# A fused forgetting-attention and FFN kernel: FFN groups of 384 tokens with one bank for layer 1 and three for layer 2, and q and k in two halves of one tile

## The chip, the cores and the metric

The kernel runs on one core of a Trainium2 chip, as one launch. The metric is the device time of that launch in microseconds. The core's engines run side by side, each with its own queue in order: TensorE (PE; its weight loads are listed apart as PEld), VectorE (DVE), ScalarE (ACT), GpSimd (POOL) and SyncE (SP), which issues all DMAs here. TensorE writes its results into eight banks of PSUM, from which DVE and ACT read them.

## The reference, cut to what matters

```python
# q, k, v: (8, 8, 576, 64), f: (8, 8, 576); w_in: (512, 2048), w_out: (2048, 512), all float32
scores = (q @ k.T) / sqrt(64)
cum = cumsum(log(clip(f, 1e-4, 1)))
scores = where(causal, -1e9, scores + cum[:, None] - cum[None, :])
attn = exp(scores - max(scores)); attn = attn / (sum(attn) + 1e-9)
x = (attn @ v) as 4608 tokens of 512            # 8 heads side by side
h = x @ w_in
out = maximum(0.01 * h, h) @ w_out
```

Products are computed to more than one float32r pass: an operand is split into a high part (`..h`, rounded to float32r) and a low part (`..l`, the rest), and high·high, low·high and high·low are summed.

## The kernel before

**Attention.** The first 256 query rows of three batches are done in an early part, two heads at a time (`early_load`, `early_scores`, `early_values`), while the weights are loaded and split. Then 64 tasks follow, one for each head: for the three early batches the rest of the rows, for the five others all 576. The loop over `t` at line 704 does in one turn the scores of task `t` (line 375: matmuls into `sc`, a maximum on DVE, an exponential on ACT into a fixed tile `z0` to `z4`), and for task `t - 1` the transposes (line 417: PE into `tr`, ACT casts into `ph`, DVE subtracts into `pl`) and the values (line 482: matmuls into `av`, ACT copies one half of the partitions into `y`, DVE adds the other half to it into `x`). After every second task `inverse` (line 510) turns the sums of both heads into factors, sends them through DRAM (`rows_d`) and broadcasts them into `main` and `rest`, and `normalise` (line 534) multiplies `x` by both and stores it to `xd` in DRAM. `load(t + 1)` (line 240) fetches q, k and, for each pair of heads, v; q and k are loaded twice each, into both halves of the partitions of `qraw` and `kraw`. `split(t + 1)` (line 352) makes float32r tiles of them: `s1` and `m1` are cast on ACT, `s2` gets its upper half by a DMA out of `s1`, POOL subtracts (`minus`) for the low parts, and `vs` is made of `vm` in the same way. `qraw`, `kraw` and `vm` have one buffer each, `s1` and `m1` two.

**FFN.** The 4608 tokens are taken in 18 groups of 256 (`ffn`, line 574). A group is read back from `xd` (`fetch_group`), split (`split_group`), and then done in 8 steps `p`. A step is 2 x 12 layer-1 matmuls of 256 columns into one tile `h`, which takes a bank (2 buffers); ACT's Prelu makes `g` of it, DVE casts `gh`, POOL (DVE after the last task) subtracts `gl`; and `second` (line 625) does the 2 x 6 layer-2 matmuls of 512 columns of the step before into two accumulators `o0` and `o1`, a bank each.

**What sets the order.** The FFN is a generator that yields after each quantum: 12 layer-1 matmuls, or 6 of layer 2. `fill` (line 657) is called some 8 times in each turn of the task loop and draws quanta by a credit. How many a turn gets is set at lines 710 to 712: the quanta of the groups whose tokens are ready, less those used, over the turns to the next end of a batch plus 3, at most 9. A scheduler then orders each engine's instructions, and puts the waits in.

Of the kernel before, what the change touches and what calls it, by code (L numbers as in the profile page):

```python
# [19 lines left out]
PARTS = (("part0", 1), ("part1", 1), ("ost", 2), ("ost", 2))  # L20
# [17 lines left out]
def forgetting_attention_ffn(ctx, tc, qT, kT, v4, vr, f, w_in, w_out, out):  # L38
# [18 lines left out]
    NG = NTOK // T  # L57
# [66 lines left out]
    eye = one.tile([P, P], F32, tag="y", name="eye")  # L124
# [4 lines left out]
    both = one.tile([P, P + T + NHEAD], F32R, tag="kraw", name="both")  # L129
# [110 lines left out]
    def load(t):  # L240

        s, c0, c1 = tasks[t]
        h = state[t] = {}
        a, n = c0 * P, S
        for name, src, lo in (("q", qT, a), ("k", kT, 0)):
            x = h[name] = one.tile([P, S], F32, tag=f"{name}raw", name=f"{name}raw_{t}")
            for o in range(2):
                nc.sync.dma_start(x[o * D:(o + 1) * D, lo:n], src[s][:, lo:n])
# [87 lines left out]
    def fix():  # L336

        for x in "ab":
            for w, n in (("s2", 2), ("m2", 4)):
# [4 lines left out]
            nc.gpsimd.memset(y, 1.0)
        for i in range(NCH):
            z = fixed[f"z{i}"] = one.tile([P, (i + 1) * P], F32, tag=f"z{i}", name=f"fixed_z{i}")
            nc.gpsimd.memset(z if i == 0 else z[:, i * P + REST:], 0.0)
        vs = fixed["vs"] = one.tile([P, 2, NCH, 2 * D], F32R, tag="vs", name="fixed_vs")
        vm = fixed["vm"] = one.tile([P, 2, NCH, D], F32, tag="vm", name="fixed_vm")
        nc.gpsimd.memset(vm[:, :, NFULL], 0.0)  # L350

    def split(t):


        s, c0, c1 = tasks[t]
        h = state[t]
        a, n = c0 * P, S
        x = "ab"[t % 2]
        s1 = h["s1"] = one.tile([P, S], F32R, tag="s1", name=f"s1_{t}", bufs=2)
        m1 = h["m1"] = one.tile([P, S], F32R, tag="m1", name=f"m1_{t}", bufs=2)  # L360
        s2, m2 = h["s2"], h["m2"] = fixed["s2" + x], fixed["m2" + x]
        nc.scalar.copy(s1[:, a:n], h["q"][:, a:n])  # L362
        nc.scalar.copy(m1[:, :n], h["k"][:, :n])
# [9 lines left out]
        nc.gpsimd.tensor_copy(vs[REST:, NFULL], vs[:REST, NFULL].bitcast(F32))

    def scores(t, i):
# [9 lines left out]
        for x, (a, b) in enumerate(parts):  # L385
# [96 lines left out]
    def values(t, part):  # L482
# [12 lines left out]
        for n, (w, j) in enumerate(steps):  # L495
# [8 lines left out]
        y = one.tile([P, 512], F32, tag="y", name=f"y_{t}_{part}")  # L504
        nc.scalar.copy(y[mine, :hi - lo], ps[other, :hi - lo])
        nc.vector.tensor_tensor(
            x[mine, lo:hi], ps[mine, :hi - lo], y[mine, :hi - lo], op=ALU.add
        )

    def inverse(t):  # L510
# [10 lines left out]
        rest = one.tile([P, 2 * P], F32, tag="part1", name=f"rbr_{t}")  # L521
        flat = rest[:2 * NCH, P:]
# [51 lines left out]
    def ffn():  # L574
# [4 lines left out]
        for at, (n, p0, p1) in enumerate(order):  # L579
            while (n + 1) * T > ready[0]:  # L580
                yield False
            if n not in groups:
# [3 lines left out]
                while n not in groups:  # L586
                    yield False
            acc = [None, None]
            for p in range(p0, p1):
                while len(loaded) < 2 * (p + 1):  # L590
                    yield False
# [3 lines left out]
                    (x, c, w, xx) for c in range(NCC)  # L595
                    for x, (w, xx) in enumerate(((win_h[p], xh), (win_l[p], xh), (win_h[p], xl)))
# [13 lines left out]
                g = one.tile([P, 2, T], F32, tag="b2", name=f"g_{n}_{p}", bufs=B2)  # L610
                nc.scalar.activation(g, ph, AF.Prelu, alpha=0.01)  # L611
                gh = one.tile([P, 2, T], F32R, tag="b2", name=f"gh_{n}_{p}", bufs=B2)
                gl = one.tile([P, 2, T], F32R, tag="b2", name=f"gl_{n}_{p}", bufs=B2)
# [11 lines left out]
    def second(n, p, p0, p1, gh, gl, acc):
        for k in range(T // P):
            if p == p0:
                acc[k] = psum.tile([P, DM], F32, tag=f"o{k}", name=f"o_{n}_{k}_{p}", bufs=1)
            ts = slice(k * P, (k + 1) * P)
            for e in range(2):  # L630
                fc_ = 2 * p + e
                for x, (gg, w) in enumerate(((gh, wout_h[p]), (gh, wout_l[p]), (gl, wout_h[p]))):
                    matmul(
                        acc[k], gg[:, e, ts], w[:, e, :],
                        start=(fc_ == 2 * p0 and x == 0), stop=(fc_ == 2 * p1 - 1 and x == 2),
                    )
            if p == p1 - 1 < NFC // 2 - 1:
# [3 lines left out]
            elif p == p1 - 1:  # L641
# [15 lines left out]
    def fill(n):  # L657
# [17 lines left out]
    TRI = S  # L675
# [28 lines left out]
    for t in range(nt + 1):  # L704
# [5 lines left out]
        have = ready[0] // T * NQ - used[0]  # L710
# [60 lines left out]
```

## Time and profile before

| | |
|---|---|
| median of 3 runs | 1210.32 us (1210.28 to 1213.06) |
| the profiled execution | 1209.1 us |
| its span | 1207.3 us |
| TensorE busy | 1187.3 us, 98% of the span |
| DVE, ACT, POOL busy | 626.7, 631.6, 462.7 us |
| TensorE clock granted | full throughout |
| DMA engines | 92 GB/s in the mean |

Span and busy times are from the profiler on the chip. Matmuls are pipelined, and the ends shown for them overlap the starts of the next; the time that one takes from TensorE is read from start to start. A wait is put down to what came last.

### The profile page before, as it was taken

What the parts mean: (1) busy time and instruction counts of PE and PEld (TensorE: products, weight loads), DVE (VectorE), ACT (ScalarE), POOL (GpSimd) and SP (SyncE); (2) the same over time, 40 slices, a digit from 0 to 9 for tenths busy, and PEclk for the clock granted to TensorE, in tenths of its full rate; (3) what the DMA queues carried; (4) which work ended last, traced back from release to release, by engine and by line L of the source; (5) the groups of instructions that cost most, each with busy time, mean ns of one, the idle gap of its engine ahead of it and who ended that gap; (6) DMA issues with size and microseconds to landing.
All of it is one profiled execution on the core that took longest, in us unless ns stands there. A gap on an engine that the chain in (4) does not pass through costs nothing.

```text
span 1207.3 us, 22237 instructions
## 1 busy us (share of the span) xinstructions
PE 1187.3 (98%) x7812; PEld 1065.9 (88%) x7812; DVE 626.7 (52%) x1687; ACT 631.6 (52%) x1633; POOL 462.7 (38%) x471
## 2 busy tenths in 40 slices
PE   9899989999999999999999999999999999999998
PEld 6678878988899999999999999999999999899997
DVE  5988646666665554454544444445443434553221
ACT  6886446757765565555544545455444445551111
POOL 0000245664455444454445354444454543631000
PEclk9999999999999999999999999999999999999999
DMA  5555323334342233323322323231223222211000
GB/s 171 197 188 171 101 84 111 98 108 135 106 134 81 79 98 97 107 79 97 98 90 61 90 71 96 74 96 52 73 85 93 58 75 76 73 57 47 18 18 18
DMA packets 81104, 110.53 MB, mean 92 GB/s; under 512 B 19617, under 2 KB 50705, under 8 KB 80993
## 3 DMA queue, kind: packets, MB, share of 16 engines
q1 hardware_dynamic: 80992, 109.11, 29.6%
q8 instruction: 62, 1.02, 0.3%
q14 instruction: 50, 0.40, 0.1%
HBM read 82.62 MB, written 18.58 MB: 84 GB/s over the span
## 4 chain that ended last, share of the span: by engine, by line
PE 88%; DVE 4%; DMA 3%; ACT 2%; issue 1%; SPq 1%; POOL 1%; ACTq 0%; POOLq 0%; DVEq 0%
PE h L108 32%; PE o L108 30%; PE tr L112 8%; PE av L108 7%; PE sc L108 7%; PE sce L108 2%; PE warm L108 1%; PE ave L108 1%; DMA wraw<-in_w_in 1%; DMA qraw<-in_qT 1%; DMA kraw<-in_kT 1%; ACT fixed_z L399 1%; DVE fixed_z L393 1%; DVE pl L445 0%; ACT ph L443 0%
## 5 line engine op out<-in xcount | busy, mean ns | idle before, releaser
L616 POOL TENSOR_TENSOR gl<-g,gh 128x512 fp32r<-128x512 f32 x111 | 145.5, 1311 | 286.8 <-DVE gh L614 266.7
L108 PE MATMUL o<-wout_h,gh 128*128 128x512 f32 x576 | 230.3, 400 | 0.0
L108 PE MATMUL o<-wout_l,gh 128*128 128x512 f32 x576 | 226.3, 393 | 0.0
L108 PE MATMUL o<-wout_h,gl 128*128 128x512 f32 x576 | 225.6, 392 | 0.0
L399 ACT ACTIVATE fixed_z<-fixed_z,max 128x192 f32<-128x192 f32 (+3 forms) x272 | 161.0, 592 | 106.7 <-DVE max L393 103.3
L108 PE MATMUL h<-xh,win_h 128*128 128x256 f32 x1152 | 207.8, 286 | 0.4 <-ACT xh L331 0.4
L393 DVE CUSTOM_DVE_ANT_0 fixed_z<-sc,tri 128x192 f32<-128x192 f32 (+3 forms) x272 | 122.6, 452 | 151.0 <-PE sc L108 148.1
L108 PE MATMUL h<-xh,win_l 128*128 128x256 f32 x1152 | 200.4, 283 | 0.4 <-DVE win_l L190 0.4
L611 ACT ACTIVATE g<-h 128x512 f32<-128x512 f32 x144 | 85.8, 596 | 217.4 <-PE h L108 206.8
L443 ACT CAST ph<-tr 128x192 fp32r<-128x192 f32 (+3 forms) x360 | 126.3, 373 | 132.9 <-PE tr L112 97.3
L614 DVE CAST gh<-g 128x512 fp32r<-128x512 f32 x144 | 75.2, 522 | 204.2 <-ACT g L611 202.6
L445 DVE TENSOR_TENSOR pl<-tr,ph 128x384 fp32r<-128x384 f32 (+3 forms) x296 | 137.9, 468 | 78.1 <-ACT ph L443 77.5
L108 PEld LDWEIGHTS h<-xh,win_h 128*128 128x128 f32 x1152 | 170.9, 190 | 6.0 <-ACT xh L331 0.9
L108 PEld LDWEIGHTS h<-xh,win_l 128*128 128x128 f32 x1152 | 165.0, 190 | 1.2 <-DVE win_l L190 0.6
L108 PE MATMUL h<-xs,win_h 128*128 128x256 f32 x1024 | 164.5, 283 | 0.0
L149 POOL TENSOR_TENSOR s<-qraw,s 64x576 fp32r<-64x576 f32 (+1 forms) x64 | 79.6, 1244 | 213.0 <-ACT s L362 213.0
L112 PE MATMUL tr<-ident_r,fixed_z 128*128 128x128 f32 x888 | 145.7, 274 | 9.4 <-POOL fixed_z L405 4.4
L108 PEld LDWEIGHTS h<-xs,win_h 128*128 128x128 f32 x1024 | 141.1, 192 | 0.0
L112 PEld LDWEIGHTS tr<-ident_r,fixed_z 128*128 128x128 f32 x888 | 107.1, 140 | 32.5 <-POOL fixed_z L405 5.7
L108 PEld LDWEIGHTS o<-wout_h,gl 128*128 128x128 f32 x576 | 108.2, 188 | 23.7 <-issue 0.2
L108 PEld LDWEIGHTS o<-wout_l,gh 128*128 128x128 f32 x576 | 108.8, 189 | 15.0 <-issue 0.2
L108 PEld LDWEIGHTS o<-wout_h,gh 128*128 128x128 f32 x576 | 108.7, 189 | 15.0
(111 smaller groups left out, 1727.7 us busy)
## 6 DMA issues: line engine op xcount, KB each, us to landing
kraw<-in_kT SPq DMA_DIRECT2D x128, 144.0 KB
qraw<-in_qT SPq DMA_DIRECT2D x80, 144.0 KB
wraw<-in_w_in SPq DMA_DIRECT2D x16, 512.0 KB
wraw<-in_w_out SPq DMA_DIRECT2D x16, 512.0 KB
fixed_vm<-in_v SPq DMA_DIRECT2D x32, 256.0 KB
xs<-xd SPq DMA_DIRECT2D x16, 512.0 KB
out<-ost SPq DMA_DIRECT2D x28, 256.0 KB
xd<-x SPq DMA_DIRECT2D x20, 288.0 KB
```

Of the source, the lines that this page charges most:

```text
L108: nc.tensor.matmul(*args, **kw)
L112: nc.tensor.transpose(*args)
L149: nc.gpsimd.tensor_tensor(out, a, b, op=ALU.subtract)
L393: nc.vector.tensor_tensor_reduce(out=z[:, a:b], in0=ps[:m, :b - a], in1=tri[:m, at:at + b - a], scale=-SCALE, scalar=3.0e38 if x == 0 else ...
L399: nc.scalar.activation(z, z, AF.Exp, bias=h["max"][:m, last:last + 1], scale=-1.0, accum_out=fixed["sum" + "ab"[s // 2 % 2]][:m, i, s % 2: ...
L443: nc.scalar.copy(strided(ph, run), source(ps, run))
L445: nc.vector.tensor_tensor(strided(pl, run), source(ps, run), strided(ph, run).bitcast(F32), op=ALU.subtract)
L611: nc.scalar.activation(g, ph, AF.Prelu, alpha=0.01)
L614: nc.vector.tensor_copy(gh, g)
L616: eng.tensor_tensor(gl, g, gh.bitcast(F32), op=ALU.subtract)
```

## The change

1. The FFN takes groups of 256 for the first four groups, then eight of 384, then two of 256: 14 groups. A wide group has 16 steps of 12 layer-1 matmuls of 384 columns into one bank `h`, and 9 layer-2 matmuls of 512 columns into three accumulators `o0` to `o2`. The narrow groups use the banks `h` and `o2` in turn for layer 1. The generator yields the cost of a piece in quanta (0.75 for half a wide layer-1 tile, 0.5 for three layer-2 matmuls) instead of True.
2. `load` fetches q into the lower and k into the upper half of the partitions of one tile `raw`. `split` casts each half, and DMAs copy `s1` into its own upper half and into `s2`, and `m1` into its lower half. POOL's subtraction for `m2` stands ahead of that for `s1`.
3. `vm` holds one head and is loaded for each task.
4. The values' copies on ACT go into `x` itself; `y` is gone. `rest` lies behind the other columns of `ph`, and the row sums pass through `main`.
5. Smaller buffers: `tri` is 448 wide instead of 576; the identity, `both` and one partial result lie in the buffers `part0` and `s1`.
6. The number of quanta that are ready is counted by group boundaries.

```diff
-PARTS = (("part0", 1), ("part1", 1), ("ost", 2), ("ost", 2))
+PARTS = (("part0", 1), ("s1", 2), ("ost", 2), ("ost", 2))
...
-    NG = NTOK // T
+    TW = 384
+    sizes = [T] * 4 + [TW] * ((NTOK - 6 * T) // TW) + [T] * 2
+    NG = len(sizes)
+    first = [sum(sizes[:n]) for n in range(NG + 1)]
...
+    def bank():
+
+        banks[0] += 1
+        return ("h", "o2")[banks[0] % 2]
...
-        for name, src, lo in (("q", qT, a), ("k", kT, 0)):
-            x = h[name] = one.tile([P, S], F32, tag=f"{name}raw", name=f"{name}raw_{t}")
-            for o in range(2):
-                nc.sync.dma_start(x[o * D:(o + 1) * D, lo:n], src[s][:, lo:n])
-        if s % 2 == 0:
-            g = s // 2
-            vm = fixed["vm"]
-            nc.sync.dma_start(vm[:, :, :NFULL], v4[g])
-            nc.sync.dma_start(vm[:REST, :, NFULL], vr[g])
-            pairs[s // 2, c0] = {}
+        x = h["raw"] = one.tile([P, S], F32, tag="qraw", name=f"raw_{t}")
+        nc.sync.dma_start(x[:D, a:n], qT[s][:, a:n])
+        nc.sync.dma_start(x[D:, :n], kT[s][:, :n])
+        g, o = s // 2, s % 2
+        vm = fixed["vm"]
+        nc.sync.dma_start(vm[:, :NFULL], v4[g][:, o])
+        nc.sync.dma_start(vm[:REST, NFULL], vr[g][:, o])
...
-        nc.scalar.copy(s1[:, a:n], h["q"][:, a:n])
-        nc.scalar.copy(m1[:, :n], h["k"][:, :n])
-        nc.sync.dma_start(s2[D:, a:n].bitcast(F32), s1[D:, a:n].bitcast(F32))
+        raw = h["raw"]
+        nc.scalar.copy(s1[:D, a:n], raw[:D, a:n])
+        nc.scalar.copy(m1[D:, :n], raw[D:, :n])
+        for y in (s1, s2):
+            nc.sync.dma_start(y[D:, a:n].bitcast(F32), s1[:D, a:n].bitcast(F32))
+        nc.sync.dma_start(m1[:D, :n].bitcast(F32), m1[D:, :n].bitcast(F32))
...
-        minus(s1[:D, a:n], h["q"][:D, a:n], s1[:D, a:n].bitcast(F32))
-        minus(m2[D:, :n], h["k"][D:, :n], m1[D:, :n].bitcast(F32))
+        minus(m2[D:, :n], raw[D:, :n], m1[D:, :n].bitcast(F32))
+        minus(s1[:D, a:n], raw[:D, a:n], s1[:D, a:n].bitcast(F32))
...
-                h[w] = one.tile([P, PTW], F32R, tag=w, name=f"{w}_{t}")
+                h[w] = one.tile([P, PTW + P], F32R, tag=w, name=f"{w}_{t}")
...
-        y = one.tile([P, 512], F32, tag="y", name=f"y_{t}_{part}")
-        nc.scalar.copy(y[mine, :hi - lo], ps[other, :hi - lo])
+        nc.scalar.copy(x[mine, lo:hi], ps[other, :hi - lo])
         nc.vector.tensor_tensor(
-            x[mine, lo:hi], ps[mine, :hi - lo], y[mine, :hi - lo], op=ALU.add
+            x[mine, lo:hi], ps[mine, :hi - lo], x[mine, lo:hi], op=ALU.add
         )
...
-        rest = one.tile([P, 2 * P], F32, tag="part1", name=f"rbr_{t}")
-        flat = rest[:2 * NCH, P:]
+        rest = state[t]["ph"][:, PTW:].bitcast(F32)
+        flat = main[:2 * NCH, :P]
...
+            step = 1 if w > T else 2
+            for f0 in range(2 * p0, 2 * p1, step):
+                p = f0 // 2
...
-                ph = psum.tile([P, 2, T], F32, tag="h", name=f"h_{n}_{p}")
-                for e in range(2):
-                    fs = slice(e * P, (e + 1) * P)
-                    for y, (x, c, w, xx) in enumerate(terms):
+                ph = psum.tile(
+                    [P, step, w], F32, tag="h" if w > T else bank(), name=f"h_{n}_{f0}", bufs=1
+                )
+                for f in range(f0, f0 + step):
+                    fs = slice(f % 2 * P, (f % 2 + 1) * P)
+                    for y, (x, c, wt, xx) in enumerate(terms):
                         matmul(
-                            ph[:, e, :], w[:, c, fs], xx[:, c, :],
+                            ph[:, f - f0, :], wt[:, c, fs], xx[:, c, :],
                             start=y == 0, stop=y == len(terms) - 1,
                         )
-                    if e == 0:
-                        yield True
+                        if w > T and y == len(terms) // 2 - 1:
+                            yield w / T / 2
+                    if f < f0 + step - 1:
+                        yield 1
...
-            credit[0] -= 1
-            if not next(quanta, None):
+            cost = next(quanta, None)
+            if not cost:
                 credit[0] = 0
                 return
-            used[0] += 1
+            credit[0] -= cost
+            used[0] += cost
...
-    TRI = S
+    TRI = PST
...
-        have = ready[0] // T * NQ - used[0]
+        have = max(x for x in first if x <= ready[0]) // T * NQ - used[0]
```

How instructions stand on the engines, before and after, at three places. The listings name tiles by task or group; they show order and waits, not times.

TensorE, from the end of the values of task 19 to the first scores of task 21 (`av`, `tr`, `sc` are attention's, `h` and `o` the FFN's, of group 4). Before:

```order
L108 MATMUL h_4_5_4863<-xh_4_4250,win_h_5_103 128x256 x4
L108 MATMUL h_4_5_4863<-xh_4_4250,win_l_5_111 128x256 x4
L108 MATMUL h_4_5_4863<-xs_4_4119,win_h_5_103 128x256 x4
L108 MATMUL o_4_0_0_4498<-wout_h_4_118,gh_4_4_4806 128x512
L108 MATMUL o_4_0_0_4498<-wout_l_4_126,gh_4_4_4806 128x512
L108 MATMUL o_4_0_0_4498<-wout_h_4_118,gl_4_4_4807 128x512
L108 MATMUL o_4_0_0_4498<-wout_h_4_118,gh_4_4_4806 128x512
L108 MATMUL o_4_0_0_4498<-wout_l_4_126,gh_4_4_4806 128x512
L108 MATMUL o_4_0_0_4498<-wout_h_4_118,gl_4_4_4807 128x512
L112 MATMUL tr_20_0_4931<-ident_r_94,fixed_z0_1717 128x128
L112 MATMUL tr_20_0_4931<-ident_r_94,fixed_z1_1719 128x128
L108 MATMUL sc_21_0_0_4937<-m1_21_4886,s1_21_4885 128x64
```

Now:

```order
L111 MATMUL av_19_1_4682<-ph_19_4563,fixed_vs_1727 128x128
L111 MATMUL av_19_1_4682<-pl_19_4564,fixed_vs_1727 128x128
L111 MATMUL o_4_1_0_4576<-wout_h_0_114,gh_4_1_4535 128x512
L111 MATMUL o_4_1_0_4576<-wout_l_0_122,gh_4_1_4535 128x512
L111 MATMUL o_4_1_0_4576<-wout_h_0_114,gl_4_1_4536 128x512
L111 MATMUL o_4_2_0_4594<-wout_h_0_114,gh_4_1_4535 128x512
L111 MATMUL o_4_2_0_4594<-wout_l_0_122,gh_4_1_4535 128x512
L111 MATMUL o_4_2_0_4594<-wout_h_0_114,gl_4_1_4536 128x512
L115 MATMUL tr_20_0_4717<-ident_r_94,fixed_z0_1717 128x128
L115 MATMUL tr_20_0_4717<-ident_r_94,fixed_z1_1719 128x128
L111 MATMUL sc_21_0_0_4723<-m1_21_4691,s1_21_4690 128x64
```

Before, 12 `h` and 6 `o` matmuls stood between the last `av` and `tr_20`; now 6 `o` do, and group 4 is at its second step where it was at its sixth.

POOL, the split of task 14 (`s1`, `m2` and `vs` are the low parts' subtractions). Before:

```order
L149 TENSOR_TENSOR s1_14_3650<-qraw_14_3532,s1_14_3650 64x576 [waits DMAHW5_49,DMAHW4_49,Activation_49]
L149 TENSOR_TENSOR fixed_m2a_1704<-kraw_14_3535,m1_14_3651 64x576 [waits PE_49,DMAHW7_49,Activation_49,Pool_49]
L405 COPY fixed_z4_1725<-fixed_z4_1725 64x64 [waits Activation_49]
L149 TENSOR_TENSOR fixed_vs_1727<-fixed_vm_1728,fixed_vs_1727 128x5x64 [waits PE_49,Activation_49,Pool_49]
L373 CAST fixed_vs_1727<-fixed_vs_1727 64x128 [waits Pool_49]
```

Now:

```order
L158 TENSOR_TENSOR fixed_m2a_1704<-raw_14_3510,m1_14_3624 64x576 [waits PE_49,DMAHW3_49,Activation_49,Pool_49]
L416 COPY fixed_z4_1725<-fixed_z4_1725 64x64 [waits Activation_49]
L158 TENSOR_TENSOR fixed_vs_1727<-fixed_vm_1728,fixed_vs_1727 128x5x64 [waits DMAHW0_49,PE_49,DMAHW1_49,Activation_49,Pool_49]
L384 CAST fixed_vs_1727<-fixed_vs_1727 64x128 [waits Pool_49]
L158 TENSOR_TENSOR s1_14_3623<-raw_14_3510,s1_14_3623 64x576 [waits DMAHW2_49,DMAHW1_49]
```

The subtraction for `s1` moved from the first place to the last, and waits for DMAs.

ACT, the end of the values of task 11 and the first cast for task 12. Before:

```order
L505 COPY y_11_0_3477<-av_11_0_3467 64x448 [waits PE_49,Activation_49]
L505 COPY y_11_1_3496<-av_11_1_3493 64x128 [waits DVE_49,PE_49]
L371 CAST fixed_vs_1727<-fixed_vm_1728 128x5x64
L611 ACTIVATE g_3_2_3526<-h_3_2_3480 128x512 [waits PE_49,Pool_49]
L443 CAST ph_12_3540<-tr_12_0_3542 128x192 [waits PE_49]
```

Now:

```order
L515 COPY x_10_3286<-av_11_0_3445 64x448 [waits PE_49]
L515 COPY x_10_3286<-av_11_1_3470 64x128 [waits PE_49]
L382 CAST fixed_vs_1727<-fixed_vm_1728 128x5x64 [waits DMAHW1_49,DMAHW0_49]
L633 ACTIVATE g_3_4_3504<-h_3_4_3457 128x512 [waits PE_49,Pool_49]
L454 CAST ph_12_3515<-tr_12_0_3517 128x192 [waits DMAHW0_49,DVE_49,DMAHW7_49,PE_49,Activation_49]
```

The second copy lost its wait for DVE, and the cast into `ph` got one for DVE and DMAs.

More of the change, by code (lines that the diff above doesn't have):

```diff
@@ L114, in forgetting_attention_ffn @@
     warmed = []
+    banks = [0]
+    def bank():
+        banks[0] += 1
+        return ("h", "o2")[banks[0] % 2]
     def warm(n):
-        ps = psum.tile([P, 512], F32, tag="h", name=f"warm_{len(warmed)}")
+        ps = psum.tile([P, 512], F32, tag=bank(), name=f"warm_{len(warmed)}", bufs=1)
         warmed.append(n)
@@ L123, in forgetting_attention_ffn @@
     warm(WARM[0])
-    eye = one.tile([P, P], F32, tag="y", name="eye")
+    eye = one.tile([P, P], F32, tag="part0", name="eye")
     make_identity(nc, eye)
@@ L128, in forgetting_attention_ffn @@
     ident = ident_r.bitcast(F32)
-    both = one.tile([P, P + T + NHEAD], F32R, tag="kraw", name="both")
+    both = one.tile([P, P + T + NHEAD], F32R, tag="s1", name="both", bufs=2)
     pick = both[:, P + T:]
@@ L348, in fix @@
         vs = fixed["vs"] = one.tile([P, 2, NCH, 2 * D], F32R, tag="vs", name="fixed_vs")
-        vm = fixed["vm"] = one.tile([P, 2, NCH, D], F32, tag="vm", name="fixed_vm")
-        nc.gpsimd.memset(vm[:, :, NFULL], 0.0)
+        vm = fixed["vm"] = one.tile([P, NCH, D], F32, tag="vm", name="fixed_vm")
+        nc.gpsimd.memset(vm[:, NFULL], 0.0)
     def split(t):
@@ L561, in fetch_group @@
     def fetch_group(n):
-        if n not in groups and n not in staged and (n + 1) * T <= ready[0]:
-            xs = staged[n] = one.tile([P, NCC, T], F32R, tag="b4", name=f"xs_{n}", bufs=B4)
+        if n not in groups and n not in staged and first[n + 1] <= ready[0]:
+            xs = staged[n] = one.tile([P, NCC, sizes[n]], F32R, tag="b4", name=f"xs_{n}", bufs=B4)
             since[n] = work[0]
-            nc.sync.dma_start(xs.bitcast(F32), xd[:, n * T:(n + 1) * T].rearrange("(c p) t -> p c t", p=P))
+            nc.sync.dma_start(
+                xs.bitcast(F32), xd[:, first[n]:first[n + 1]].rearrange("(c p) t -> p c t", p=P)
+            )
     def split_group(n):
         xs = staged[n]
-        xh = one.tile([P, NCC, T], F32R, tag="b4", name=f"xh_{n}", bufs=B4)
+        xh = one.tile([P, NCC, sizes[n]], F32R, tag="b4", name=f"xh_{n}", bufs=B4)
         tc.keep_in_program_order(nc.vector.tensor_copy(xh, xs.bitcast(F32)))
@@ L579, in ffn @@
         for at, (n, p0, p1) in enumerate(order):
-            while (n + 1) * T > ready[0]:
-                yield False
+            w = sizes[n]
+            while first[n + 1] > ready[0]:
+                yield 0
             if n not in groups:
@@ L594, in ffn @@
                 terms = [
-                    (x, c, w, xx) for c in range(NCC)
-                    for x, (w, xx) in enumerate(((win_h[p], xh), (win_l[p], xh), (win_h[p], xl)))
+                    (x, c, wt, xx) for c in range(NCC)
+                    for x, (wt, xx) in enumerate(((win_h[p], xh), (win_l[p], xh), (win_h[p], xl)))
                 ]
@@ L616, in ffn, with second @@
                 eng.tensor_tensor(gl, g, gh.bitcast(F32), op=ALU.subtract)
-                yield True
+                yield w / T / 2 if w > T else 1
                 if pending is not None:
                     yield from second(*pending)
-                if p0 < p and at + 1 < len(order):
+                if 2 * p0 < f0 and at + 1 < len(order):
                     fetch_group(order[at + 1][0])
-                pending = (n, p, p0, p1, gh, gl, acc)
+                pending = (n, f0, step, p0, p1, gh, gl, acc)
         yield from second(*pending)
[L625 to L628, printed above, removed]
+    def second(n, f0, step, p0, p1, gh, gl, acc):
+        for k in range(sizes[n] // P):
+            if f0 == 2 * p0:
+                acc[k] = psum.tile([P, DM], F32, tag=f"o{k}", name=f"o_{n}_{k}_{f0}", bufs=1)
             ts = slice(k * P, (k + 1) * P)
-            for e in range(2):
-                fc_ = 2 * p + e
+            for f in range(f0, f0 + step):
+                e, p = f - f0, f // 2
                 for x, (gg, w) in enumerate(((gh, wout_h[p]), (gh, wout_l[p]), (gl, wout_h[p]))):
                     matmul(
-                        acc[k], gg[:, e, ts], w[:, e, :],
-                        start=(fc_ == 2 * p0 and x == 0), stop=(fc_ == 2 * p1 - 1 and x == 2),
-                    )
-            if p == p1 - 1 < NFC // 2 - 1:
+                        acc[k], gg[:, e, ts], w[:, f % 2, :],
+                        start=(f == 2 * p0 and x == 0), stop=(f == 2 * p1 - 1 and x == 2),
+                    )
+            end = f0 + step == 2 * p1
+            if end and p1 < NFC // 2:
                 tag, m = PARTS[2 * n + k]
@@ L647, in second @@
                     nc.scalar.copy(o, acc[k])
-                for x, row, m in segments(n * T // P + k):
+                for x, row, m in segments(first[n] // P + k):
                     nc.sync.dma_start(out[row:row + m, :], o[x:x + m])
-            yield True
+            yield step / 2
     parts = {}
```

23 lines of the change are left out of this document (13 added, 10 removed).

## The prediction

> **What bounds the kernel now.** I read the page first, then busy time by stretches, then TensorE's rows in one pure FFN stretch, then the chain of waits where TensorE idles. The page:
>
> ```profile
> span 1207.3 us, 22237 instructions
> ...
> PE 1187.3 (98%) x7812; PEld 1065.9 (88%) x7812; DVE 626.7 (52%) x1687; ACT 631.6 (52%) x1633; POOL 462.7 (38%) x471
> ```
>
> TensorE leaves some 20 us free, so time can only come from its own instructions or from those 20 us. Busy time by stretches tells where they lie (columns: stretch, its length, then busy us of PE, its weight loads, DVE, ACT, POOL, each with its instructions, then granted clock, DMA share and rate):
>
> ```profile
> core 0: us, PE busy (x) PEld busy (x) DVE busy (x) ACT busy (x) POOL busy (x), PEclk, DMA share, GB/s
> 156.00:250.00 94.00, 89.04 (x597) 80.30 (x597) 58.63 (x168) 59.84 (x160) 50.37 (x54) 1.00 0.33 96
> 250.00:337.00 87.00, 82.56 (x561) 73.97 (x560) 54.66 (x168) 59.04 (x168) 47.72 (x48) 1.00 0.38 112
> 337.00:457.00 120.00, 119.34 (x810) 109.62 (x809) 67.65 (x193) 69.77 (x190) 58.67 (x57) 1.00 0.34 100
> 457.00:1000.00 543.00, 542.45 (x3654) 500.08 (x3654) 250.76 (x720) 271.22 (x713) 245.57 (x235) 1.00 0.27 82
> 1000.00:1080.00 80.00, 79.90 (x536) 72.69 (x535) 42.50 (x118) 44.93 (x118) 38.49 (x43) 1.00 0.26 77
> 1080.00:1207.00 127.00, 123.67 (x788) 111.84 (x786) 33.07 (x66) 21.45 (x44) 7.60 (x5) 1.00 0.07 24
> ```
>
> From 337 us on TensorE is the bound: 0.7 us idle in 120, 0.5 in 543. From 156 to 337 us, where tasks follow each other with little FFN work between, it idles 5.0 us in 94 and 4.4 us in 87, some 5%. I call that part the dense stage.
>
> **Layer 1, the gain.** The pure FFN stretch gives the price of one matmul from starts, since busy times overlap:
>
> ```profile
> 1144.62 0.64 PE L108 MATMUL h<-xh,win_h 128*128 128x256 f32 x4
> ...
> 1147.02 0.64 PE L108 MATMUL h<-xs,win_h 128*128 128x256 f32 x4
> 1147.49 0.40 PE L108 MATMUL o<-wout_h,gh 128*128 128x512 f32 x1
> ...
> 1148.88 0.39 PE L108 MATMUL o<-wout_h,gh 128*128 128x512 f32 x1
> ...
> 1150.02 0.39 PE L108 MATMUL o<-wout_h,gl 128*128 128x512 f32 x1
> 1150.24 0.28 PE L108 MATMUL h<-xh,win_h 128*128 128x256 f32 x1
> ```
>
> Six rows of four, 24 `h` matmuls, take 1147.49 - 1144.62 = 2.87 us, 119.6 ns each; the 12 `o` matmuls up to 1150.24 take 2.75 us, 229 ns each. The line through both is 10 ns a matmul and 0.427 ns a column. The columns stay the same in all; twelve groups of 192 matmuls (2304) become eight of 192 (1536). No row shows N = 384: by the line one takes 174.3 ns, and the saving is 2304 x 119.6 - 1536 x 174.3 = 7.8 us. Bounds from the same rows: the six `o` before 1148.88 take 232 ns, the six behind 227; with these the line gives 175.8 and 173.3 ns, 5.5 and 9.4 us. I take **-7.8 us**, the mean line. Layer 2 keeps its 1728 matmuls of 512 columns, nine to a step instead of twelve.
>
> [...]
>
> **One bank for layer 1.** Until now the next `h` tile had a second bank; in a wide group its first matmul waits for the Prelu of the last. Nine `o` matmuls stand between, 9 x 0.229 = 2.06 us at least. Of the page, the groups of instructions that evacuate `h` (behind the second bar: idle time of the engine before them, and what ended it):
>
> ```profile
> L616 POOL TENSOR_TENSOR gl<-g,gh 128x512 fp32r<-128x512 f32 x111 | 145.5, 1311 | 286.8 <-DVE gh L614 266.7
> ...
> L611 ACT ACTIVATE g<-h 128x512 f32<-128x512 f32 x144 | 85.8, 596 | 217.4 <-PE h L108 206.8
> ...
> L614 DVE CAST gh<-g 128x512 fp32r<-128x512 f32 x144 | 75.2, 522 | 204.2 <-ACT g L611 202.6
> ```
>
> ACT mostly idles until the matmuls are there (206.8 us in all), and then needs 0.6 us, less for 384 columns: done 1.4 us early. `gl` is needed after those 2.06 us and the next `h` (12 x 0.1743 = 2.1), 4.2 us plus the two matmuls with `gh`; Prelu, cast and subtraction take 0.6 + 0.5 + 1.3 = 2.4 us. Price 0; a Prelu queued behind more than 1.4 us of other ACT work costs what is over (rival C). The 32 more Prelus, casts and subtractions lie on engines half idle from 337 us on.
>
> **The dense stage grows.** The pacing at `have` counts whole groups that are ready, 32 quanta each. When 1664 tokens are ready that was 6 groups; now the last boundary is 1408, and 1408 // 256 = 5. That is 32 quanta less over left + SLACK = 8 + 3 tasks, 2.9 per task, and a quantum is 12 `h` or 6 `o`, 1.4 us. The listings agree: between the first score matmuls of tasks 20 and 21 stood 48 `h` and 24 `o` (11.2 us), now 12 wide `h` and 15 `o` (5.5 us); from task 17 to task 25 some 79 us of FFN become 46. So the stretch 337 to 457 shrinks by 33 to about 87 us and looks like 250 to 337: 4.4 us idle instead of 0.7, **+3.7 us**. The 33 us of FFN come later, into stretches without idle time. Bounds: -0.7, if the stretch keeps no idle time at all, and 4.4, if its 0.7 us don't come off.
>
> **Attention part by part.** The chain of waits in the dense stage:
>
> ```profile
> 289.20 0.53 ACT y L505
> ...
> 289.76 0.64 DVE x L506
> ...
> 290.48 0.27 ACT y L505
> ...
> 290.76 0.31 DVE x L506
> ...
> 291.70 0.89 DVE x L541
> ...
> 292.63 0.22 DVE fixed_z L393
> ```
>
> The second copy into `y` waited for the first addition, since `y` has one buffer; all waits of that kind:
>
> ```profile
> ACT y L505 <- DVE x L506: 11.5, 15, 3.7
> ACT m L363 <- DMA kraw<-in_kT: 6.1, 4, 2.8
> ```
>
> Now the copies go into `x` itself and needn't: the second addition starts at 290.42 instead of 290.76, 0.34 us earlier on a chain that ends in the next task's maxima, and ACT is free 0.7 us sooner. Tasks 8 to 25 (two parts each, dense) make 18 x 0.34 = 6 us at most, 0 if another wait takes over; I take half, **-3 us**.
>
> The remainder of `inverse` moves into `ph`. So after every second task the next task's first cast into `ph` waits for the multiplication by it, and the exponentials behind that cast on ACT wait too. ACT around the same place:
>
> ```profile
> 287.01 0.67 ACT L362 CAST s<-qraw 128x576 fp32r<-128x576 f32 x1
> 287.59 0.68 ACT L363 CAST m<-kraw 128x576 fp32r<-128x576 f32 x1
> 288.31 0.78 ACT L399 ACTIVATE fixed_z<-fixed_z,max 128x576 f32<-128x576 f32 x1
> ...
> 292.21 0.31 ACT L443 CAST ph<-tr 128x192 fp32r<-128x192 f32 x1
> ...
> 298.19 0.67 ACT L362 CAST s<-qraw 128x576 fp32r<-128x576 f32 x1
> ```
>
> The small multiplication (the chain's row at 291.70) ends at 292.59, the cast began at 292.21: 0.4 us late. Half of tasks 1 to 25 by 0.4 us make 5 us at most, 0 at least; the 0.34 us that the chain gained come off each, so I take **+0.5 us**.
>
> Loads: `raw` is one buffer, freed by the later of two subtractions, where `qraw` and `kraw` were freed apart. POOL at task 14:
>
> ```profile
> 287.76 1.44 POOL L149 TENSOR_TENSOR s<-qraw,s 64x576 fp32r<-64x576 f32 x1 [4.79 <-ACT s L362]
> 289.28 1.43 POOL L149 TENSOR_TENSOR fixed_m2a<-kraw,m 64x576 fp32r<-64x576 f32 x1
> ...
> 291.35 1.17 POOL L149 TENSOR_TENSOR fixed_vs<-fixed_vm,fixed_vs 128x320 fp32r<-128x320 f32 x1 [0.46 <-POOL fixed_z L405]
> 292.58 0.29 POOL L373 CAST fixed_vs<-fixed_vs 64x128 fp32r<-64x128 f32 x1
> ```
>
> The subtraction for `s1` now comes last, at about 292.9 to 294.3, behind `m2`, `vs` and the copies of `s1` out of its upper half; SP then issues two loads (it took 1.2 us for the two of `kraw`):
>
> ```profile
> 295.13 1.23 SPq L248 DMA_DIRECT2D kraw<-in_kT x2
> ```
>
> So they leave at 295.5, and the next cast out of `raw` is due at 298.19: 2.7 us for the data. The three copies inside SBUF replace two loads from HBM; they land more than a task before the scores that read them, and what waits on POOL for them stands behind `m2` and `vs` (3 us). Price 0 to 1 us per dense task; I take 1 us in all. The start (identity, `both`, partial result in other buffers) and a narrower `tri` move nothing that TensorE waits for in a row: 0, bounds -2 and +2.
>
> **Sum.** -7.8 + 3.7 - 3 + 0.5 + 1 = -5.6 us. The profiled execution took 1209.1 us and becomes 1203.5; the median of the runs is 1.2 us higher, so **1204.7 us**.
>
> **Rivals.**
>
> A, the whole gain: 9.4 us from layer 1, the dense stage's idle time cured by the free `x` copies (-6) and its growth costing half (1.9): -13.5, **1196.8 us**. For it: the six chain rows above. Against it: the chain passes other engines too. Chance 0.17.
>
> B, no gain in layer 1: a matmul's time goes wholly with its columns, so one of 384 takes 1.5 x 119.6 = 179.4 ns, and 1536 of them as long as 2304 before. The other terms make +2.2: **1212.5 us**. Against it: at 512 that would be 239 ns, and the rows have 229. Chance 0.07. [...]
>
> C, the single bank: Prelu queues behind two casts and an exponential (0.67 + 0.68 + 0.78 us), 0.7 us over the 1.4. Seven dense tasks are wide, with 5.5 us of FFN each and 4.2 us to a step, so some nine Prelus: 9 x 0.7 = 6.4 us, **1211.4 us**. It decides once ACT is over 1.4 us late. Against it: attention matmuls nearly always stand between as well. Chance 0.10.
>
> D, slower: the load of `raw`. ACT's casts stand in order, so a late load stops the exponentials behind them. A load has been that late:
>
> ```profile
> 244.67 3.06 DMA xd<-x
> ...
> 248.73 5.66 DMA kraw<-in_kT
> ...
> 254.41 0.68 ACT m L363
> ```
>
> There a queue in order and a crowded transfer took 5.66 us, against the 2.7 now left: 3 us too late. It decides from 2.7 us on; at 3.2 us in each of 25 dense tasks the loss is 25 x 0.5 = 12.5 us: **1217 us**. Against it: half the bytes are loaded, and only 4 casts waited before, 6.1 us in all. Chance 0.18.
>
> The forecast holds the remaining 0.48. That the matmuls don't become fewer is excluded by the listing: 1536 of 384 columns and 1152 of 256.
>
> **How the numbers follow.** A measurement here tells 0.3% (3.6 us) from no change, so faster is under 1206.7 and slower over 1213.9. The forecast's own range is 1200 to 1209; 0.36 of its 0.48 lies under 1206.7, and A adds 0.17: faster 0.53. Same: 0.12 of the forecast, 0.05 of B, 0.07 of C, 0.02 of D: 0.26. Slower: 0.16 of D, 0.03 of C, 0.02 of B: 0.21. From 1196 to 1216, about half of A and two thirds of D are left out, 0.2.
>
> **What would show it.** In the profile after: twelve wide `h` matmuls taking 2.08 to 2.11 us from start to the next `o` (2.15 would be B); TensorE at 5% idle through tasks 17 to 25, then under 1% to the end; no wait of `y` for `x` on ACT; waits of ACT's casts for `raw` under 3 us in all (over 10: D); waits of `h` matmuls for ACT `g` under 1 us (over 5: C). Wrong, above all, if idle time after the dense stage rises: then a wait that I priced at nothing sits in the steady part.

## The result: 0.8% slower

The changed kernel takes 1221.15 us (median of 6 runs, 1218.38 to 1223.41), the kernel before 1211.79 us over its 6 runs beside it: 1.0077 times as long, with a 95% interval from 1.0061 to 1.0094, some 9.3 us. I had forecast 1204.7 us and a range up to 1216. Both the sign and the range were wrong.

The page after, and busy time by the same stretches as before (columns as in the prediction):

```profile
span 1216.6 us, 21061 instructions
...
PE 1186.8 (98%) x7044; PEld 1056.3 (87%) x7044; DVE 648.5 (53%) x1720; ACT 640.8 (53%) x1665; POOL 460.6 (38%) x494
```

```profile
156.00:250.00 94.00, 89.08 (x587) 80.41 (x586) 56.74 (x168) 60.66 (x159) 49.98 (x55) 0.98 0.38 103
250.00:337.00 87.00, 82.94 (x557) 73.21 (x557) 55.05 (x170) 59.71 (x167) 45.45 (x47) 1.00 0.40 109
337.00:457.00 120.00, 112.63 (x677) 100.53 (x677) 77.72 (x222) 75.18 (x215) 64.21 (x63) 0.99 0.40 112
457.00:1000.00 543.00, 540.14 (x3096) 492.50 (x3094) 267.86 (x739) 279.70 (x740) 250.76 (x259) 1.00 0.29 82
1000.00:1080.00 80.00, 78.62 (x454) 71.94 (x454) 37.91 (x107) 38.65 (x99) 31.25 (x38) 1.00 0.20 55
1080.00:1217.00 137.00, 132.37 (x797) 119.65 (x795) 33.99 (x62) 21.66 (x42) 6.04 (x4) 1.00 0.07 24
```

TensorE has 768 matmuls less and is busy just as long (part of that is the clock, below); it idles 29.8 us instead of 20.0. Most of the new idle time lies in two places: from 337 to 457 us, 7.4 us instead of 0.7, and from 457 to 1080 us, 4.2 us (2.86 + 1.38) instead of 0.65. From 156 to 337 us it didn't grow (9.0 us, before 9.4); behind 1080 us it is 4.6 us instead of 3.3.

The longer and fewer matmuls are there, but they are worth half of what I thought. Two steps in the pure FFN stretch after (start, length, then the row; the steps repeat every 4.18 us):

```profile
1099.88 0.87 PE L111 MATMUL h<-xh,win_h 128*128 128x384 f32 x4
...
1101.98 0.39 PE L111 MATMUL o<-wout_h,gh 128*128 128x512 f32 x1
...
1104.06 0.87 PE L111 MATMUL h<-xh,win_h 128*128 128x384 f32 x4
...
1116.62 0.87 PE L111 MATMUL h<-xh,win_h 128*128 128x384 f32 x4
```

Twelve `h` matmuls take 2.10 us, 175.0 ns each (I had 174.3), and the nine `o` matmuls behind them 2.08 us, 231 ns each, where they had 229 among narrow groups. Four steps take 16.74 us, 4.185 each. Before, a step of 24 `h` and 12 `o` took 5.62 us. The wide tokens need 12 x 8 such steps before, 539.5 us, and 8 x 16 after, 535.7 us: **3.8 us** gained, where I had 7.8 and a lower bound of 5.5.

One caution on the two profiles: the profile of before shows the full clock, that of after 0.997 (the 0.98 and 0.99 above), which alone is 3.6 us of their distance. So 9.8 us of idle time, 3.8 us of work saved and 3.6 us of clock make up the distance of these two. Over the runs the clock matters less: its mean is 0.9966 for before (18 runs of the first set of experiments; the 6 runs above have no clock on record) and 0.9958 for after (6 runs), a difference of 1 us. As far as is known, then, the clock explains little of the 9.3 us between the medians, and 2 to 3 us of these aren't located.

### The profile page after: what moved, and what is told of

The parts are those of the page before. It is cut to its first block, busy times and chain, and to the rows that moved or that the text cites. A ratio compares the mean times of both kernels' runs of the same rounds, so it can differ in the third digit from the quotient of the medians.

```text
span 1216.6 us, 21061 instructions
## 1 busy us (share of the span) xinstructions
PE 1186.8 (98%) x7044; PEld 1056.3 (87%) x7044; DVE 648.5 (53%) x1720; ACT 640.8 (53%) x1665; POOL 460.6 (38%) x494
## 4 chain that ended last, share of the span: by engine, by line
PE 79%; DVE 6%; ACT 5%; DMA 4%; issue 3%; POOL 2%; SPq 1%; ACTq 0%; POOLq 0%; DVEq 0%
PE h L111 29%; PE o L111 27%; PE tr L115 7%; PE av L111 6%; PE sc L111 6%; PE sce L111 2%; ACT fixed_z L410 2%; PE warm L111 1%; DVE pl L456 1%; PE ave L111 1%; ACT ph L454 1%; DMA raw<-in_qT 1%; DVE gh L634 1%; ACT g L633 1%; DMA wraw<-in_w_in 1%
## 5 line engine op out<-in xcount | busy, mean ns | idle before, releaser
L636 POOL TENSOR_TENSOR gl<-g,gh 128x384 fp32r<-128x384 f32 (+1 forms) x138 | 146.7, 1063 | 252.0 <-DVE gh L634 245.2
L634 DVE CAST gh<-g 128x384 fp32r<-128x384 f32 (+1 forms) x176 | 103.8, 590 | 230.6 <-ACT g L633 229.7
L633 ACT ACTIVATE g<-h 128x384 f32<-128x384 f32 (+1 forms) x176 | 91.3, 518 | 236.6 <-PE h L111 201.8
L111 PE MATMUL h<-xh,win_l 128*128 128x384 f32 (+1 forms) x896 | 202.2, 317 | 0.4 <-DVE win_l L199 0.4
L111 PE MATMUL h<-xh,win_h 128*128 128x384 f32 (+1 forms) x896 | 193.5, 318 | 0.4 <-ACT xh L339 0.4
L111 PEld LDWEIGHTS h<-xh,win_h 128*128 128x128 f32 x896 | 152.1, 190 | 10.4 <-ACT xh L339 0.9
L111 PE MATMUL h<-xs,win_h 128*128 128x384 f32 (+1 forms) x768 | 151.6, 319 | 0.0
L111 PEld LDWEIGHTS h<-xh,win_l 128*128 128x128 f32 x896 | 150.1, 190 | 1.5 <-DVE win_l L199 0.6
L111 PEld LDWEIGHTS h<-xs,win_h 128*128 128x128 f32 x768 | 126.6, 190 | 0.0
L111 PE MATMUL sc<-m,s 128*128 128x288 f32 (+1 forms) x336 | 120.7, 364 | 0.1
```

Of the source, the lines that this page charges most:

```text
L111: nc.tensor.matmul(*args, **kw)
L634: nc.vector.tensor_copy(gh, g)
L636: eng.tensor_tensor(gl, g, gh.bitcast(F32), op=ALU.subtract)
```

## Experiments: how much FFN work each task is given

Theory 1 is the pacing step of my prediction with another size: rounding down whole groups leaves tasks 17 to 25 too little FFN work. Rivals: the new attention code, or the wide groups by themselves (their longer instructions on GpSimd, the single bank). All ratios are to the kernel before, beside which they ran. "Quanta per task" is worked out by carrying the program's own pacing arithmetic through: from task 17 to task 25 the kernel before does 175 - 119 = 56 quanta, 7.0 a task, the changed one 150.5 - 119 = 31.5, 3.9 a task. The matmuls in the two profiles, counted between the same casts as below, make 52 and 32.

**The old count back.**

```diff
-        have = max(x for x in first if x <= ready[0]) // T * NQ - used[0]
+        have = ready[0] // T * NQ - used[0]
```

> The changed kernel with one line put back: the pacing counts 256-token units that are ready, as before the change, instead of whole groups. Theory 1 (thin FFN supply in tasks 17 to 25 causes the loss): idle time of TensorE from 337 to 457 us falls from 7.4 us to 1-2 us, the halved clock there goes away, and the time falls by 6 to 10 us from 1221 to 1211-1215. Rival (the loss sits in the attention edits or in VectorE waiting for GpSimd, wherever the tasks stand): 0 to 3 us less.

Measured: 1226.87 us, ratio 1.0115 (1.0098 to 1.0132), slower still. Tasks 17 to 25 were cured (the first row, TensorE idle 1.2 us), but the stretch of tasks 25 to 33 (the second) now idled 5.5 us. Busy time by stretches, and the chain of waits in the second stretch:

```profile
320.77:435.17 114.40, 113.17 (x696) 103.36 (x695) 66.00 (x193) 69.34 (x193) 55.39 (x57) 1.00 0.36 96
435.17:563.12 127.95, 122.47 (x705) 110.70 (x705) 71.39 (x199) 71.81 (x195) 61.86 (x61) 0.99 0.34 94
```

```profile
470.18 3.46 POOL xs L158
473.64 0.04 issue
473.69 0.98 PE h L111 x4
```

The count promises tokens of a group that isn't complete yet. TensorE runs out of groups and then waits for the next one's subtraction, 3.46 us on GpSimd; the waits of `h` for it came to 7.5 us in three places, 1.9 us of them in this stretch. The longest gap of the stretch, 2.55 us up to 457.98 us, was another: transposes waited for VectorE's `pl`, with no FFN matmul to run meanwhile. Half of the expectation held, the time went the other way: the new count had kept the kernel from the wait for an unfinished group. The test had to be one that changes only the rounding.

**The exact count.**

```diff
-        have = max(x for x in first if x <= ready[0]) // T * NQ - used[0]
+        have = max(x for x in first if x <= ready[0]) * NQ / T - used[0]
```

> The changed kernel with the pacing counting exactly what whole groups hold (1408 tokens are 176 quanta, not 160), neither rounded down as in the change nor counting tokens of an unfinished group as in the run with the old count. Theory 1, narrowed (too few quanta in tasks 17 to 25, but a count beyond the last whole group makes TensorE wait for the next group's rows): idle time from 337 to 457 us falls from 7.4 to 3-5 us, no wait of h matmuls for xs of 1 us or more, time 2 to 5 us less than the changed kernel. Rival (any count that runs earlier only moves the wait): within 1 us of it, with new waits of h matmuls for the group's rows.

Measured: 1209.93 us, ratio 0.9981 (0.9966 to 0.9995). A rounding of 16 quanta, which bites wherever a group ends on an odd multiple of 128, carried the whole loss, and more than I expected: 0.96% between the two ratios, 11.6 us. In the two profiles TensorE idles 23.5 us instead of 29.8, 6.3 us less; the mean granted clock of the runs (0.9973 against 0.9958) is worth another 1.8 us; where the rest lies the traces don't show. Tasks 17 to 25 get 5.5 quanta each. Idle time there, for the kernels before, changed, and with the exact count, each from the cast of `s` for task 17 to that for task 25:

```profile
320.44:436.35 115.91, 114.73 (x780) 105.33 (x779) 66.55 (x190) 69.01 (x192) 57.55 (x55) 1.00 0.35 102
```

```profile
320.50:417.71 97.21, 89.07 (x558) 79.63 (x557) 64.22 (x185) 64.27 (x185) 49.31 (x50) 0.98 0.41 113
```

```profile
324.56:428.26 103.70, 100.77 (x627) 90.70 (x626) 64.33 (x190) 67.11 (x189) 53.51 (x54) 1.00 0.39 106
```

1.2, 8.1 and 2.9 us, for 7.0, 3.9 and 5.5 quanta a task. This version beats both kernels, by little.

**Thin supply in the old kernel.** Whether thin supply needs the wide groups to hurt, the kernel before can tell, with nothing of the change in it:

```diff
-        have = ready[0] // T * NQ - used[0]
+        have = (ready[0] // T - (ready[0] == 1664)) * NQ - used[0]
```

> The kernel before the change, untouched but for its pacing: while 1664 tokens are ready it counts one group of 256 less, 41 quanta left at task 17 instead of 73, as the changed kernel did (151 done by task 25 instead of 175). Attention code, groups, banks and buffers are the old ones. Theory 1 (the thin supply alone makes the loss): idle time between tasks 17 and 25 rises from 1.2 us to 6-9 us, and the time by 4 to 8 us, 1.003 to 1.007 times before. Rival (thin supply hurts only together with the wide groups or the new attention code): within 0.2% of before, idle time there under 4 us.

Measured: 1216.91 us, ratio 1.0048 (1.0030 to 1.0065): 5.8 us lost by the count alone, as expected. Idle time between tasks 17 and 25 was 5.4 us, less than the 6 to 9 expected:

```profile
321.55:415.58 94.03, 88.65 (x598) 78.88 (x597) 61.23 (x188) 63.53 (x184) 50.78 (x50) 1.00 0.41 119
```

So thin supply is cause enough of a loss, though the changed kernel's is larger. What it lets through is seen on ACT, in the run with the old code and thin supply, and in the changed kernel:

```profile
346.33 0.67 ACT L363 CAST m<-kraw 128x576 fp32r<-128x576 f32 x1 [1.78 <-DMA kraw<-in_kT]
```

```profile
345.59 0.67 ACT L372 CAST m<-raw 64x576 fp32r<-64x576 f32 x1 [2.21 <-DMA raw<-in_kT]
```

The same load of `k` is late at the same place, with two raw tiles and with one. My reading is that tasks that follow each other too fast overtake their loads; TensorE then idled over 2 us in both: 2.10 us up to 349.35 us in the old code, 2.12 us up to 348.60 us in the changed kernel.

**Wide groups one group later**, so that groups end on 1664, 2816 and 3968 tokens:

```diff
-    sizes = [T] * 4 + [TW] * ((NTOK - 6 * T) // TW) + [T] * 2
+    sizes = [T] * 5 + [TW] * ((NTOK - 6 * T) // TW) + [T]
```

> The changed kernel, its pacing line untouched, with the eight wide groups starting one group later (five narrow, eight wide, one narrow). Group ends then fall on 1664, 2816 and 3968 tokens, where attention has just finished that many: the same line yields 73 quanta left at task 17 (before the change 73, in the changed kernel 41) and 175 quanta done by task 25 (175; 150). Theory 1: the loss vanishes without touching the pacing, idle time from 337 to 457 us under 2 us, 0.995 to 0.999 times before. [...]

> The same with the exact count. It supplies tasks 17 to 24 with 89 quanta instead of 73. If more supply still helps there: 0.1 to 0.3% below the run with the shift alone. If 73 is enough: within 0.1% of it. Both keep only some 30 quanta for tasks 57 to 63 (52 before the change), so idle time from 1000 us on may grow by 1 to 2 us.

Measured: 1.0017 (1.0004 to 1.0030) with the pacing line untouched, 1.0043 (1.0027 to 1.0059) with the exact count. The shift takes away most of the loss of 0.77%, and the stretch from task 17 to 25 idles 1.5 us (first row), but the result is above what I expected: tasks 57 to 63 now get 2.9 quanta each (5.2 before) and idle 2.9 us (second row).

```profile
323.37:439.45 116.08, 114.56 (x765) 105.37 (x764) 67.88 (x192) 69.48 (x192) 58.42 (x55) 1.00 0.38 104
...
970.53:1038.92 68.39, 65.45 (x385) 57.96 (x384) 36.64 (x109) 40.25 (x108) 32.09 (x40) 1.00 0.32 87
```

The exact count on top was expected to be level or better and was 0.26% worse: it spends quanta early, and its two largest gaps after 200 us, 1.86 us each, came behind a long cast on VectorE at 766 us (2.67 us until the next instruction there; such casts are below) and before a group's remainder that came late, from 1099 us on. Which share each has is not settled. More supply early is no cure in general; that it would have to be even is a guess that no run tests.

## Experiments: GpSimd's subtraction, the attention edits, later wide groups

In the changed kernel 35 of the 176 casts of `g` on VectorE took over 0.7 us (the usual is 0.36 us for 384 columns, 0.43 for 512), against 13 of 144 before. The worst (3.25, 3.22 and 3.08 us) lie beside the wide group's subtraction. GpSimd, VectorE and TensorE around 742 us:

```profile
741.97 3.50 POOL L158 TENSOR_TENSOR xs<-xs,xh 128x1536 fp32r<-128x1536 f32 x1
```

```profile
742.62 3.08 DVE L634 CAST gh<-g 128x384 fp32r<-128x384 f32 x1 [1.85 <-ACT g L633]
745.61 0.35 DVE L456 TENSOR_TENSOR pl<-tr,ph 128x192 fp32r<-128x192 f32 x1
```

```profile
746.07 0.27 PE L115 MATMUL rt<-ident_r,r 128*10 128x128 f32 x1
747.65 0.41 PE L115 MATMUL tr<-ident_r,fixed_z 128*128 128x128 f32 x2 [1.31 <-DVE ph L461]
```

The cast ends at 745.70 us, 0.23 us after the subtraction (745.47 us); `pl` is queued behind it, and TensorE idles 1.3 us. Theory 2 was that this makes the loss.

```diff
-        minus(xs, xs.bitcast(F32), xh.bitcast(F32))
+        for c in range(NCC):
+            minus(xs[:, c], xs[:, c].bitcast(F32), xh[:, c].bitcast(F32))
```

> The changed kernel with the group's remainder (xs minus xh on GpSimd, one instruction of 3.5 us in a wide group) split into four instructions, one for each 128 rows (0.9 us each). Theory 2 (a cast on VectorE stands still until GpSimd's subtraction ends, and the wide group's is 1.1 us longer): no cast of g takes over 1.6 us any more, the five gaps of TensorE behind such casts (about 6 us in all) shrink, and the time falls by 2 to 6 us. Rival (the long casts lie beside other waits): within 1 us of the changed kernel.

Measured: 1217.82 us, ratio 1.0038 (1.0024 to 1.0052), 4.7 us less than the changed kernel by the two ratios. The gain doesn't lie in the dense stage: from task 17 to 25 TensorE idles 8.9 us, in the changed kernel 8.1; one cast still took 3.93 us there (last section), with a gap of 2.53 us behind it. From 457 to 1080 us it idles 1.9 us instead of 4.2. With the exact count:

> Exact count and split subtraction together, eight wide groups. If the two causes are separate, their gains add: split alone gave some 4 us in ratio (1.0077 to 1.0038), so 1.000 to 1.002 times before. If they are the same gaps, no better than the split alone: 1.003 to 1.005.

Measured: 0.9989 (0.9975 to 1.0003), no better than the exact count alone, and below both of my answers: I had compared with the split alone, and the count was worth far more. And with the pieces given out one at a time (each filling point issues one, so that GpSimd does other work between them):

```diff
-            if n not in groups and (
+            if n in halfway and n not in groups:
+                split_piece(n)
+            elif n not in groups and (
...
```

> The changed kernel with the exact count, and the group's subtraction in four pieces given out one per filling point, with other work between them on GpSimd, instead of one instruction of 3.5 us. With the exact count the four pieces in a row gained nothing. If the long stretch on GpSimd (VectorE's casts and the remainder gl queue behind it) still costs: the remaining gaps behind it (1.8 us at 505 us, some 1 us elsewhere) go, 1 to 3 us less than the exact count alone, 0.996 to 0.9975 times before. If these gaps only close what another wait opens: 0.9975 to 0.999.

Measured: 0.9980 (0.9969 to 0.9990), again level. So the long subtraction costs some 5 us with the changed kernel's thin supply, and nothing that can be measured with the exact count. It makes thin supply dearer; by itself it isn't the cause.

**The attention edits alone** (TW = 256: all groups narrow, one raw tile, no `y`, the remainder in `ph`):

```diff
-    TW = 384
+    TW = 256
```

> The changed kernel with all 18 groups of 256 tokens: the attention edits (one raw tile, no y, the remainder in ph, smaller tri) stay, the wide groups go, and with them the changed pacing and the single bank. If the attention edits cost what the widening seemed to cost, 1217-1222. If they cost or gain little, as I predicted (-1.5 us), 1208-1213, level with before, and the wide groups carry the loss of some 9 us.

Measured: 1212.33 us, ratio 0.9987 (0.9976 to 0.9998): 1.6 us gained, where the prediction's three terms make 1.5. With the split subtraction, from which theory 2 would have a gain here too (in the kernel before, four casts took 1.76 to 2.55 us beside the narrow group's subtraction of 2.4 us), and the rival next to none:

> All groups of 256 tokens with the attention edits, and the subtraction split into four. [...] Rival (in the narrow kernel TensorE is fed anyway): 0.998 to 0.9995.

Measured: 0.9990 (0.9977 to 1.0003): no gain, the rival. One of the edits undone in the changed kernel, the remainder in a tile of its own:

```diff
-        rest = state[t]["ph"][:, PTW:].bitcast(F32)
+        rest = one.tile([P, REST], F32, tag="rest", name=f"rest_{t}")
```

> The changed kernel with the remainder of inverse in a tile of its own (64 columns) instead of behind ph. ACT's casts into ph waited 10.2 us in six places for the multiplication by it. If these waits carry to TensorE (theory 3): 3 to 6 us less than the changed kernel. If ACT's order hides them or another wait takes their place, as my prediction had it (0.5 us): within 1 us.

Measured: 1.0062 (1.0046 to 1.0077). The interval overlaps that of the changed kernel; a gain of up to 4 us isn't excluded, and none is shown.

**Four wide groups, late** (exact count, split subtraction):

```diff
-    sizes = [T] * 4 + [TW] * ((NTOK - 6 * T) // TW) + [T] * 2
+    sizes = [T] * 10 + [TW] * ((NTOK - 12 * T) // TW) + [T] * 2
```

> Ten narrow groups, then four wide, then two narrow, with exact count and split subtraction. Theory (the wide groups lose in the dense stage up to 457 us, and gain some 0.6 us each elsewhere): below the narrow kernel with the split by 1 to 3 us. Rival (wide groups lose wherever they stand, through VectorE and GpSimd): 1 to 4 us above it.

Measured: 0.9993 (0.9977 to 1.0008), level with the narrow groups (0.9990) and with eight wide ones (0.9989). Neither answer: wide groups neither gain nor lose clearly once the supply is right. Their 3.8 us at most would show as 0.3%; the profile of the exact count idles 3.6 us more than that of the narrow kernel (19.8 and 16.2 us up to 1080 us), so it seems that most of the gain goes into waits again.

## Why the prediction was wrong, step by step

**Layer 1, -7.8 us.** Right kind, twice too large: -3.8 us. The line put an `h` of 384 columns at 174.3 ns, measured 175.0; that is 1.1 us over 1536 matmuls. Layer 2, which I kept at its old price, costs more: 128 times 2.08 us against 96 times 2.75, 2.2 us. The remaining 0.7 us is within what rows of 0.01 us can tell over 128 steps.

**The dense stage, +3.7 us.** This is the step that failed. The mechanism was the right one, the place too (tasks 17 to 25, 5 groups counted for 6), but not the size: idle time rose by 6.7 us from 337 to 457 us, outside my bound of 4.4, and half of those 32 quanta, the rounding, was worth 11.6 us of time. I had taken the price from the stretch at 250 to 337 us, as if the same quanta a task (3.6 to 4.4 there by the matmuls) meant the same idle time. In the old kernel that was nearly right (1.2 to 5.4 us idle from task 17 to 25), though the time rose by 5.8. The changed kernel idles 8.1 us there at the same supply. Of the difference, one gap of 1.62 us stands behind a cast on VectorE that took 3.25 us beside the first wide group's subtraction (352.14 to 355.61 us on GpSimd):

```profile
352.64 3.25 DVE L634 CAST gh<-g 128x512 fp32r<-128x512 f32 x1 [2.62 <-ACT g L633]
```

```profile
356.55 0.52 PE L115 MATMUL tr<-ident_r,fixed_z 128*128 128x128 f32 x3 [1.62 <-DVE ph L461]
```

I had priced the wide subtraction on GpSimd at nothing, because GpSimd was half idle; how long VectorE's casts beside it would take I hadn't asked. The shrinking of the stretch was off as well: tasks 17 to 25 became 18.7 us shorter (115.91 to 97.21), not 33, since 20 quanta less ran there and the idle time grew.

**"The 33 us of FFN come later, into stretches without idle time."** Wrong, and a term that I put at nothing: idle time from 457 to 1080 us rose from 0.65 to 4.2 us. The rounding also bites at later ends of groups, and casts that ended only after GpSimd's subtraction are there too (1.22 to 3.08 us, at 606, 742, 790 and 999 us). The last paragraph of the prediction named this as what would prove it wrong. With the exact count 1.9 us of these are gone (2.2 us idle from 457 to 1000 us, then 0.1), with the split subtraction 2.3.

**Attention, -3 + 0.5 + 1.** Right in the sum, -1.6 measured with narrow groups (-2.9 to -0.2). That it fits so well is partly luck, since the waits behind two of the three parts came out larger than I had put them. All waits of the changed kernel on the disputed places (us in total, how many, the longest):

```profile
ACT ph L454 <- DVE x L551: 10.2, 6, 3.1
...
ACT s L371 <- DMA raw<-in_qT: 4.6, 4, 1.5
ACT m L372 <- DMA raw<-in_kT: 4.4, 5, 2.2
...
PE h L111 <- ACT xh L339: 0.4, 1, 0.4
PE h L111 <- DVE win_l L199: 0.4, 1, 0.4
```

No wait of `y` for `x` is left, as said. Waits for `raw` are 9.0 us, three times the 3 that I allowed, though the old kernel waited 7.5 us for `qraw` and `kraw` (1.4 + 6.1); waits of the cast into `ph` for the multiplication are 10.2 us, where I took 0.5. In the narrow kernel, where the attention and the buffers alone are new, these waits are 4.5 and 5.4 us and don't cost more than the `x` copies gain. How much each part gained or lost isn't shown.

**The rivals.** A (1196.8) and B (1212.5) are out: the gain in layer 1 is there, but half. C is out: the rows above have all waits of `h` matmuls, and none is for ACT's `g`. (Its terms add up to 1211.1 us, 1204.7 + 6.4, not 1211.4; nothing hangs on it.) D had the right side, 1217, and the wrong reason: the loads of `raw` do come late at times, but in the old kernel with thin supply one of the two raw tiles was late at the same place, 1.78 us against 2.21. What was missing among the rivals is the one that came true: my own pacing step at three times its price.

**Range and chances.** The loss was among the terms of the sum, at a third of its size, and slower had a chance of 0.21, 0.16 of it from rival D; the range ended at 1216 because the bounds of the pacing term (-0.7 to 4.4 us) were taken from a single stretch of the same profile.

## What to carry to other kernels

Where a planner counts work in units of a tile, changing the tile changes the plan, even when the work stays the same: go through each point at which it counts, write down the units per step before and after, and look for rounding. A stage that is bound by TensorE only because filler work covers the waits has a steep price for filler taken away: here 16 quanta of 576, counted too low, cost more (11.6 us) than everything that the wide tile could bring (3.8 us). And price a longer instruction not only by its own engine's idle time but by who stands still while it runs: here a cast of 0.36 us on VectorE took 3.08 us beside a subtraction of 3.50 us on GpSimd.

## What the runs showed of the hardware

**VectorE and GpSimd.** The cast of 128x384 from f32 to fp32r takes 0.36 us and took up to 3.2 us when GpSimd was subtracting. In the changed kernel nine casts of `g` overlap a group's subtraction (`xs` minus `xh`, 2.4 us in a narrow group, 3.5 in a wide one). They took 1.22 to 3.25 us, and each ended 0.2 to 0.3 us after the subtraction, as in the rows at 742 us. With the subtraction in four pieces, 4.05 us in all, one cast still took 3.93 us, from 351.28 us, within the subtraction for `s` before them, to 355.21 us, 0.86 us before the four had ended:

```profile
350.64 1.41 POOL L158 TENSOR_TENSOR s<-raw,s 64x576 fp32r<-64x576 f32 x1
352.02 4.05 POOL L158 TENSOR_TENSOR xs<-xs,xh 128x384 fp32r<-128x384 f32 x4
```

```profile
351.28 3.93 DVE L635 CAST gh<-g 128x512 fp32r<-128x512 f32 x1 [1.40 <-ACT g L634]
```

So here the cast did not end with the first piece. Why the casts take so long beside GpSimd isn't shown by any run.

**The clock.** In the changed kernel TensorE's granted clock was 0.50 from 349.04 to 352.45 us, for 3.41 us, starting 0.44 us behind an idle gap of 2.12 us up to 348.60 us (stretches of 1 us; the clock is the third number from the end):

```profile
346.00:347.00 1.00, 0.48 (x5) 0.27 (x3) 0.00 (x0) 0.97 (x3) 0.61 (x1) 1.00 0.04 12
347.00:348.00 1.00, 0.00 (x0) 0.00 (x0) 0.79 (x3) 0.98 (x5) 0.97 (x2) 1.00 0.60 136
348.00:349.00 1.00, 0.40 (x4) 0.40 (x5) 1.00 (x4) 0.23 (x1) 0.64 (x1) 1.00 0.04 12
349.00:350.00 1.00, 1.00 (x7) 1.00 (x6) 1.00 (x4) 0.53 (x2) 1.00 (x1) 0.52 0.00 0
...
352.00:353.00 1.00, 1.00 (x9) 1.00 (x8) 0.35 (x1) 0.88 (x3) 1.00 (x2) 0.77 0.09 22
353.00:354.00 1.00, 1.00 (x7) 0.79 (x7) 1.00 (x1) 0.29 (x2) 1.00 (x1) 1.00 0.44 120
```

The same profile shows it once more before the last work, from 232.99 to 236.40 us, behind a gap of 1.70 us up to 231.78 us; over a gap of 2.22 us up to 172.93 us the clock stayed full. The profile of before idled 2.12, 1.85 and 1.85 us (up to 164.17, 175.07 and 256.34 us) and kept the full clock; so did the old kernel with thin supply over its gap of 2.10 us. A gap of this length was followed by half clock in some places and not in others; the runs don't show what decides it.
